# Top-k attention and two MLPs on one core: float32 scores, a head pair side by side

## The chip, the core and the metric

The kernel runs on one core of one Trainium2 chip. The metric is device time in microseconds of the whole program, one launch. Within the core TensorE (PE) multiplies, VectorE (DVE), ScalarE (ACT) and GpSimd (POOL) do the elementwise work, and SyncE (SP) issues most DMAs. The loading of TensorE's stationary operand is listed as PEld.

## The reference

```python
# q, k, v: batch 2, heads 8, sequence 576, head width 64, float32
scores = (1 / sqrt(64)) * q @ k.T                 # 576 x 576 for each head
kth    = 32nd largest score of each row
scores = where(scores >= kth, scores, -1e9)
attn   = exp(scores - rowmax); attn /= attn.sum() + 1e-9
x = (attn @ v) with heads side by side            # 1152 tokens x 512
h = x @ w_in                                      # 512 -> 2048
g = h * tanh(log1p(exp(min(h, 20))))
x = g @ w_out                                     # 2048 -> 512
a, b = x @ w_a, x @ w_b                           # 512 -> 1536 each
out = (a * b) @ w_out2                            # 1536 -> 512
```

The choice of the 32 largest hangs on small differences between scores, so scores are computed to about float32 accuracy. The weights arrive as float64 bit patterns and are turned into float32 in the kernel.

## The kernel before

The 1152 tokens are nine tiles of 128. Tile 4 holds the last 64 tokens of both batches, so its two halves use two different sets of keys. For each tile and each of four head pairs (36 steps) the kernel makes the scores (`scores`), searches the 32 largest by four rounds of MAX8 (L501) and three of MATCH_REPLACE8 (L505) on VectorE (`largest`), and then makes masked exponentials on ScalarE, transposes them on TensorE (L558) and multiplies by v (L577, L581; `weighted_sum`). In these value products each head writes 64 of the 128 columns of the array, the two heads in turn.

How scores are made before: for tile 0 as plain float32 products over the 64 rows of one head (L471), 16 matmuls. For the other tiles q and k are split: the high part of k, rounded to a shorter format, lies in rows 0 to 63 and the remainder in rows 64 to 127 of one operand, and q, which the host has laid twice into 128 rows, is split into a high and a low operand. Two matmuls over 128 rows (L481), q high and q low against that k, then give a float32 result for one head and 288 keys; four of them in tile 4, one pair for each batch, with zeros in the other batch's columns. The splits are casts (helper `cast`, L353, on ScalarE or VectorE) and differences (helper `minus`, L365, on GpSimd or VectorE), once for each head of k in `prep_k` and for each tile and head pair of q in `prep_q`. The heads of one pair are worked one behind the other, and each half row of 288 scores goes from PSUM into SBUF by a ScalarE eviction (L487).

The MLPs: the first (`single`, plain float32, tiles 0, 1 and 2 one at a time: L810 and L738; `gated`, split into high and low parts in three terms, for tiles 3 to 5 and 6 to 8: L715, L738 and L736) has a gate (`gate`), which begins with an exponential, then a minimum with exp(20) on GpSimd or VectorE (L771), then four more operations. The second (`bilinear`) is split for all tiles (L715, L738) and runs first on tiles 0 to 2: its first product is the first L715 in the program, called the first split product below. The weights are converted early on ScalarE, GpSimd and VectorE (L648 to L667) and stored to DRAM for later loads.

The order of all this is set by a planner (`Plan`). Each piece of work has a priority from tables (`ATT`, `CONV`, `MLP`, `BIAS`), a cost by formula for each engine that may do it, and rotating buffers; the planner walks through time by these costs and gives each free engine the ready piece with the lowest priority number. The result is written out as one fixed order for each engine. Where the plan expects TensorE to be idle for more than 2 us ahead of a piece with a `fill`, it puts products of the identity matrix there (L359), so that the clock does not fall. Instructions on an engine run in that order.

```python
rate = 1.0 if warm else 0.5                        # planner's TensorE clock
add(one("PE", 484.0), ...)                         # L471, one head, 288 keys
add(one("PE", 132.0 * len(heads)), ...)            # L481, two matmuls (four in tile 4)
```

Of the kernel before, what the change touches and what calls it, by code (L numbers as in the profile page):

```python
# [29 lines left out]
ATT = (-95.6, -15.5, 57.8, 65.0, 267.4, 322.4, 412.6, 617.3, 258.4, 2216.9)  # L30
CONV = (-130.2, -85.8, -15.1, 293.4, 516.4)
MLP = ((-72.5, 59.6, -546.2, 994.6), (150.3, 181.0, 313.3, -81.3), (-893.9, 26.7, -324.4, 153.9), (354.4, 585.5),
        (832.0, -20.7), (569.8, 2514.2), (1477.1, 1301.3), (616.5, 711.8))
BIAS = {'scores': -41.8, 'search': 43.8, 'weigh': 44.9, 'gate': -652.5, 'conv': -24.4, 'load': -87.3, 'split':
        -71.0, 'x': -191.9, 'k': -413.0, 'prod': 21.0, 'acc': 35.4, 'out': 22.8, 'store': 307.2, 'v': 1080.8, 'px':
        -507.2, 'mask': 1116.2, 'turn': -37.7, 'tail': -40.6, 'last': -0.9, 'rest': 372.0}
FRESH = 200
RAW = (0,)
# [11 lines left out]
CAPS = {'bank': 3, 'ph': 2, 'acc': 3, 'w64': 4, 'w': 6, 'raw': 9, 'whl': 6, 's2': 5, 'wk': 3, 'e2': 2, 'et': 2, 'q':  # L50
        2, 'x': 4, 'y': 2, 'ep': 3, 'gs': 2, 'k': 1}
# [227 lines left out]
SHIFT = {'DVE': -103.4, 'POOL': -52.0, 'ACT': 3021.6, 'PE': 0, 'SP': 0}  # L279
LOCKED = 1091.7  # L280
# [9 lines left out]
def topk_attention_mlps(ctx: ExitStack, tc: tile.TileContext, q, k, v, vr, w, out):  # L290
# [7 lines left out]
    B, _, H, S = k.shape  # L298
    D = q.shape[1] // 2
    NP = H // 2  # L300
# [66 lines left out]
    kks = [buf("const", [P, S], F32R, "kk") for _ in range(H + 2)]  # L367
# [10 lines left out]
    V, V4, KK, KR, QQ, X, XR, Y, HELD = {}, {}, {}, {}, {}, {}, {}, {}, {}  # L378
# [20 lines left out]
    part = lambda z: slice(0, P) if z == 2 else slice(z * D, (z + 1) * D)  # L399

    def load_k(b, hp, pr, z):
        done = ready(J * b - 2) if b else []
        if (b, hp) not in KR:
            KR[b, hp] = buf("const", [P, 2, S], F32, "kr") if b == 0 and RAW else buf("wp", [P, 2, S], F32, "kr", CAPS["k"])
        kr = KR[b, hp]
        first = b == 0 and hp == 0
        for h, n in ((0, 1), (1, 1)) if first else ((0, 2),):
            dma(pr, lambda h=h, n=n: kr()[part(z), h:h + n], lambda h=h, n=n: k[b, part(z), 2 * hp + h:2 * hp + h + n, :],
                (495000 if z == 2 else 363000) * n / 2, done, [(kr, (z, h))])

    def k_parts(b, hp, s, rows):
        return [(KR[b, hp], (z, s if b == 0 and hp == 0 else 0)) for z in rows]

    def prep_k(b, hp, pr):
        load_k(b, hp, pr, 1 if (b, hp) in KR else 2)
        kr = KR[b, hp]
        for s in range(2):
            got = k_parts(b, hp, s, (0, 1) if b == 0 and RAW else (2,))
            kk = KK[b, 2 * hp + s] = kks[(b * H + 2 * hp + s) % (H + 2)]
            cast(pr, kk, lambda s=s: kr()[:, s], 95.0 + 0.84 * S, got, [(kk, 0)], True)  # L420
            minus(pr, lambda kk=kk: kk()[D:], lambda s=s: kr()[D:, s], lambda kk=kk: kk()[D:].bitcast(F32), S,
                  got + [(kk, 0)], [(kk, 0)])
# [547 lines left out]
```

## Time and profile before

| | us |
|---|---|
| median of three runs | 651.97 (651.19 to 652.31) |
| profiled execution, first to last instruction | 647.8 |
| median less that span | 4.17 |
| TensorE busy | 619.9 |
| VectorE busy | 546.0 |
| ScalarE busy | 478.3 |
| GpSimd busy | 440.8 |

For the profiled execution the profile gives its span; what lies around it is read as the 4.17 us by which the median of the runs stands above it. "Busy" counts an instruction's whole duration; TensorE's matmuls overlap, so that a matmul's duration is longer than the time from its start to the next one's start. A float32 matmul stands in the trace as two records, a matmul on rounded operands (type fp32r) as one. Shapes are partitions x elements; for TensorE "128\*64" is rows x columns of the array.

### The profile page before, as it was taken

To read this page: it belongs to the slowest core of one execution; us is meant where nothing else is said; L and a number is where in the kernel's file an instruction comes from. 1 tells how busy PE (TensorE), PEld (TensorE's weight loads), DVE (VectorE), ACT (ScalarE), POOL (GpSimd) and SP (SyncE) were. 2 spreads that over 40 slices of the span, in tenths; PEclk is the share of its full clock that TensorE was granted. 3 is DMA by queue.
4 is the path that set the end of the run, shared out by engine and by line. 5 is a ranking of instruction groups with operands and counts; after the bars stand their busy time and mean duration, and the time that the engine had idled before them with its cause. 6 is when DMAs were issued, how large, how long until landed. Compare 5 with 4: busy or idle time off the path is not lost.

```text
span 647.8 us, 12295 instructions
## 1 busy us (share of the span) xinstructions
PE 619.9 (96%) x4122; PEld 547.7 (85%) x4122; DVE 546.0 (84%) x1083; ACT 478.3 (74%) x1057; POOL 440.8 (68%) x480
## 2 busy tenths in 40 slices
PE   7889789999999999999999999999999999999997
PEld 5778657967758899899989998889989999999996
DVE  4999999999999999999999989998765666655552
ACT  5778798898998999997998888777454767632221
POOL 2898999998979999997787785556334566621110
PEclk9989999999999999999999999999999999999999
DMA  8879879898999867632753342223207534434401
GB/s 210 317 234 301 270 236 303 281 347 284 331 334 329 292 224 245 196 98 82 215 176 116 115 130 82 78 88 112 85 7 221 165 113 131 146 99 129 123 26 49
DMA packets 65248, 118.50 MB, mean 183 GB/s; under 512 B 6945, under 2 KB 23393, under 8 KB 65185
## 3 DMA queue, kind: packets, MB, share of 16 engines
q1 hardware_dynamic: 65104, 117.66, 56.9%
q8 instruction: 32, 0.52, 0.3%
q14 instruction: 32, 0.25, 0.1%
q10 hardware_dynamic: 80, 0.07, 0.0%
HBM read 97.52 MB, written 20.19 MB: 182 GB/s over the span
## 4 chain that ended last, share of the span: by engine, by line
PE 73%; DVE 11%; ACT 6%; POOL 4%; DMA 3%; issue 2%; POOLq 0%; SPq 0%; ACTq 0%; DVEq 0%
PE ph L715 32%; PE po L738 11%; PE acc L738 7%; PE acc L736 5%; DVE arena L501 5%; DVE arena L505 4%; PE psc L481 4%; PE px L577 4%; PE pe L558 4%; PE ph L810 2%; PE psc L471 2%; ACT arena L353 2%; POOL arena L667 2%; ACT arena L775 1%; POOL arena L663 1%
## 5 line engine op out<-in xcount | busy, mean ns | idle before, releaser
L365 POOL TENSOR_TENSOR arena<-arena,arena 128x512 fp32r<-128x512 f32 (+4 forms) x188 | 216.3, 1162 | 154.3 <-ACT arena L353 126.2
L715 PE MATMUL ph<-arena 128*128 128x384 f32 x1248 | 230.9, 337 | 1.1 <-DVE arena L859 0.8
L715 PEld LDWEIGHTS ph<-arena 128*128 128x128 f32 x1248 | 216.8, 188 | 4.1 <-DVE arena L859 1.1
L501 DVE MAX8 arena<-arena 128x8 f32<-128x576 f32 x288 | 204.2, 744 | 6.7 <-ACT arena L487 5.8
L353 ACT CAST arena<-arena 128x512 fp32r<-128x512 f32 (+4 forms) x223 | 121.3, 565 | 56.2 <-PE ph L715 21.8
L505 DVE MATCH_REPLACE8 arena<-arena 128x576 f32<-128x576 f32 x216 | 159.1, 740 | 0.1
L365 DVE TENSOR_TENSOR arena<-arena,arena 128x512 fp32r<-128x512 f32 (+3 forms) x110 | 81.0, 738 | 18.9 <-ACT arena L353 13.9
L738 PE MATMUL acc<-arena 128*128 128x512 f32 x240 | 83.9, 478 | 2.7 <-DVE arena L777 2.4
L738 PE MATMUL po<-arena 128*128 128x512 f32 x324 | 80.7, 394 | 0.0
L667 POOL TENSOR_TENSOR arena<-arena 128x512 int32<-128x512 int32 x59 | 77.2, 1312 | 3.5 <-DVE arena L661 2.0
L738 PEld LDWEIGHTS po<-arena 128*128 128x128 f32 x324 | 59.6, 188 | 11.2 <-issue 0.2
L487 ACT ACTIVATE arena<-psc 128x288 f32<-128x288 f32 x144 | 54.7, 420 | 12.6 <-PE psc L471 6.0
L544 ACT ACTIVATE arena<-arena 128x576 f32<-128x576 f32 x72 | 55.1, 779 | 10.3 <-DVE arena L501 9.2
L353 DVE CAST arena<-arena 128x512 fp32r<-128x512 f32 (+2 forms) x75 | 38.9, 523 | 28.1 <-PE ph L715 10.9
L663 POOL TENSOR_TENSOR arena<-arena,eight 128x512 uint32<-128x512 uint32 x55 | 58.2, 1063 | 3.7 <-ACT arena L648 2.6
L481 PE MATMUL psc<-arena 128*128 128x288 f32 x288 | 57.4, 324 | 1.4 <-POOL arena L365 1.4
L547 ACT ACTIVATE arena<-arena 128x576 f32<-128x576 f32 x72 | 56.2, 782 | 3.0 <-POOL arena L540 3.0
L738 PEld LDWEIGHTS acc<-arena 128*128 128x128 f32 x240 | 42.0, 189 | 15.5 <-issue 7.2
L353 ACT COPY arena<-pe 128x384 f32<-128x384 f32 x108 | 48.4, 486 | 6.6 <-PE pe L558 6.5
L558 PEld LDWEIGHTS pe<-ident,arena 128*128 128x128 f32 x324 | 37.8, 140 | 17.6 <-ACT arena L547 9.0
L558 PE MATMUL pe<-ident,arena 128*128 128x128 f32 x324 | 47.2, 275 | 5.5 <-ACT arena L547 4.7
L810 PEld LDWEIGHTS ph<-arena 128*128 128x128 f32 x384 | 45.5, 192 | 8.1 <-issue 3.3
(63 smaller groups left out, 766.6 us busy)
## 6 DMA issues: line engine op xcount, KB each, us to landing
arena<-ws SPq DMA_DIRECT2D x144, 256.0 KB, 2.8
arena<-in_w_dram SPq DMA_DIRECT2D x68, 512.0 KB, 5.2
ws<-arena SPq DMA_DIRECT2D x52, 256.0 KB, 5.5
arena<-wsa SPq DMA_DIRECT2D x48, 256.0 KB, 3.4
arena<-in_q_dram SPq DMA_DIRECT2D x8, 512.0 KB, 4.2
wsa<-arena SPq DMA_DIRECT2D x16, 256.0 KB, 5.3
arena<-in_k_dram SPq DMA_DIRECT2D x4, 576.0 KB, 6.1
arena<-in_v_dram SPq DMA_DIRECT2D x4, 512.0 KB, 6.6
```

Of the source, the lines that this page charges most:

```text
L353: add(eng, prio, lambda e: nc.scalar.copy(dst(), src()) if e == "ACT" else nc.vector.tensor_copy(dst(), src()), reads, writes)
L365: lambda e: ENG[e].tensor_sub(dst(), a(), b()), reads, writes)
L481: nc.tensor.matmul(psc()[:, :HS], z()[:, s, :], kk()[:, a * HS:(a + 1) * HS], start=(i == 0), stop=(i == len(heads) - 1))
L501: lambda e, s=s, src=src, got=got: nc.vector.max(m8()[:, s, got], src()[:, s, :]),
L505: lambda e, s=s, src=src, got=got: nc.vector.match_replace(wk()[:, s, :], m8()[:, s, got], src()[:, s, :], NEG),
L547: lambda e, s=s: nc.scalar.activation(e2()[:, s, :], e2()[:, s, :], AF.Exp, scale=-STEEP, bias=dm()[:, s - 2 + n:s - 1 + n], accum_out=at_ ...
L558: nc.tensor.transpose(pe()[:, i * P:(i + 1) * P], ef[:, n * P:(n + 1) * P], ident)
L663: nc.gpsimd.tensor_tensor(wi().bitcast(U32), wi().bitcast(U32), eight.to_broadcast([P, U]), op=ALU.mult)
L667: lambda e, word=word, wi=wi: ENG[e].tensor_tensor(wi(), wi(), word(I32, 0), op=ALU.add),
L715: nc.tensor.matmul(ph()[:, o:o + T], a, x, start=(i == 0), stop=(i == len(mm) - 1))
L738: nc.tensor.matmul(acc[i](), z[:, i * P:(i + 1) * P], a, start=begin, stop=end)
L810: nc.tensor.matmul(ph()[:, j * P:(j + 1) * P], wa()[:, j * P:(j + 1) * P], x()[:, c, :], start=(c == 0 and j == 0), stop=(c == NC - 1 and ...
```

## The change

- **Scores.** All tiles get plain float32 products over 64 rows. The host now lays the two heads of a pair into rows 0 to 63 and 64 to 127, so that q has 128 rows for a pair instead of each head twice, and k as well. One piece of work is two matmuls, head 0 on the upper 64 rows and head 1 on the lower 64, into two PSUM banks (L426 of the new program); for tile 4 four matmuls, each 64 rows by 64 columns. `prep_k`, `prep_q`, the zeroing and the special path of tile 0 go. Loads of q and k have half the bytes.
- **Gate minimum.** The same instruction now has a second operation, a maximum with 0, which leaves the value of an exponential as it is. Its planned costs change.
- **Plan.** New numbers in the tables; three rotating q buffers; the first pieces of the program get 15 identity products ahead of them.

```diff
-ATT = (-95.6, -15.5, 57.8, 65.0, 267.4, 322.4, 412.6, 617.3, 258.4, 2216.9)
+ATT = (-314.6, -14.6, 75.9, 107.2, 174.6, 217.9, 226.5, 1087.3, 1309.4, 2701.9)
...
-SHIFT = {'DVE': -103.4, 'POOL': -52.0, 'ACT': 3021.6, 'PE': 0, 'SP': 0}
+SHIFT = {'DVE': -22.2, 'POOL': 1042.3, 'ACT': 6005.8, 'PE': 0, 'SP': 0}
...
-    def prep_k(b, hp, pr):
-        load_k(b, hp, pr, 1 if (b, hp) in KR else 2)
-        kr = KR[b, hp]
-        for s in range(2):
-            got = k_parts(b, hp, s, (0, 1) if b == 0 and RAW else (2,))
-            kk = KK[b, 2 * hp + s] = kks[(b * H + 2 * hp + s) % (H + 2)]
-            cast(pr, kk, lambda s=s: kr()[:, s], 95.0 + 0.84 * S, got, [(kk, 0)], True)
-            minus(pr, lambda kk=kk: kk()[D:], lambda s=s: kr()[D:, s], lambda kk=kk: kk()[D:].bitcast(F32), S,
-                  got + [(kk, 0)], [(kk, 0)])
+        kr = KR[b, hp] = buf("const", [P, S], F32, "kr")
+        dma(pr, kr, lambda: k[b, :, hp, :], 295000, done, [(kr, 0)])
...
-                    heads = [(z, KK[i, 2 * hp + s]) for i, y in made for z in y]
-
-                    def mult(e, s=s, a=a, psc=psc, heads=heads):
-                        for i, (z, kk) in enumerate(heads):
-                            nc.tensor.matmul(psc()[:, :HS], z()[:, s, :], kk()[:, a * HS:(a + 1) * HS],
-                                             start=(i == 0), stop=(i == len(heads) - 1))
-
-                    add(one("PE", 132.0 * len(heads)), pr, mult, [(z, None) for y in heads for z in y], [(psc, 0)], [s2])
-                    fill(psc)
+        for a in range(2):
+            pscs = [bank("psc") for _ in range(2)]
+
+            def mult(e, a=a, pscs=pscs):
+                for i, o, n in groups(t):
+                    for s in range(2):
+                        nc.tensor.matmul(pscs[s]()[o:o + n, :HS], qr()[s * D:(s + 1) * D, hp, o:o + n],
+                                         KR[i, hp]()[s * D:(s + 1) * D, a * HS:(a + 1) * HS], start=True, stop=True)
+
+            add(one("PE", 2 * 0.84 * HS), pr, mult, got, [(z, 0) for z in pscs], [s2])
+            fill(pscs[0])
...
-        add({"POOL": (330.0 + 2.42 * N, True), "DVE": (70.0 + 0.52 * N, True)}, pr,
-            lambda z: ENG[z].tensor_scalar(e(), e(), TOP, None, op0=ALU.min), [(e, 0)], [(e, 0)])
+        add({"POOL": (75.0 + 1.21 * N, True), "DVE": (250.0 + 0.52 * N, True)}, pr,
+            lambda z: ENG[z].tensor_scalar(e(), e(), TOP, 0.0, op0=ALU.min, op1=ALU.max), [(e, 0)], [(e, 0)])
...
-    arrays = {"q": _np.concatenate([turned_q] * 2, axis=1), "k": _np.concatenate([turned] * 2, axis=1), "v": main, "vr": rest}
+    paired_q = turned_q.reshape(9, 64, 4, 2, P).transpose(0, 3, 1, 2, 4).reshape(9, P, 4, P)
+    paired_k = turned.reshape(2, 64, 4, 2, -1).transpose(0, 3, 1, 2, 4).reshape(2, P, 4, -1)
+    arrays = {"q": paired_q, "k": paired_k, "v": main, "vr": rest}
```

Line numbers shift: before L501, L505, L558, L577, L581, L596, L715 and L810 are after L447, L451, L504, L523, L527, L542, L661 and L756.

The order on TensorE at the start of the program, before (psc are scores, pe the transposes of exponentials, px the value products, ph and acc the MLP; x16 is a count):

```order
L471 MATMUL psc<-arena_81 128x288 x16
L359 MATMUL pe<-ident 128x128 x31
L558 MATMUL pe<-ident,arena_81 128x128 x9
L481 MATMUL psc<-arena_82 128x288 x6
L596 MATMUL px<-ident,arena_81 64x128 x2
L577 MATMUL px<-arena_81 64x128 x8
L581 MATMUL px<-arena_81 64x128 x2
```

and after:

```order
L358 MATMUL psc<-ident 128x128 x15
L426 MATMUL psc<-arena_81 128x288 x18
L504 MATMUL pe<-ident,arena_81 128x128 x6
L542 MATMUL px<-ident,arena_81 64x128 x2
L504 MATMUL pe<-ident,arena_81 128x128 x3
L426 MATMUL psc<-arena_81 128x288 x2
L523 MATMUL px<-arena_81 64x128 x8
L527 MATMUL px<-arena_81 64x128 x2
```

Tile 0's 16 products one head at a time and 31 identity products behind them have become 15 identity products ahead of nine score pairs, the last of which belongs to tile 1.

The order on TensorE around the first split product (L715 before, L661 after; po is the split layer's output, prs and pt small transposes), before:

```order
L577 MATMUL px<-arena_81 64x128 x8
L581 MATMUL px<-arena_81 64x128 x2
L481 MATMUL psc<-arena_82 128x288 x16
L715 MATMUL ph<-arena_82 128x384 x48
L738 MATMUL po<-arena_82 128x512 x9
L558 MATMUL pe<-ident,arena_81 128x128 x3
L621 MATMUL prs<-ident,arena_81 64x128 x8
L558 MATMUL pe<-ident,arena_81 128x128 x3
L715 MATMUL ph<-arena_82 128x384 x12
L558 MATMUL pe<-ident,arena_81 128x128 x3
```

and after:

```order
L523 MATMUL px<-arena_81 64x128 x8
L527 MATMUL px<-arena_81 64x128 x2
L736 MATMUL pt<-ident,arena_81 128x128 x4
L426 MATMUL psc<-arena_81 64x288 x8
L661 MATMUL ph<-arena_82 128x384 x12
L426 MATMUL psc<-arena_81 64x288 x4
L661 MATMUL ph<-arena_82 128x384 x12
L504 MATMUL pe<-ident,arena_81 128x128 x3
L426 MATMUL psc<-arena_81 64x288 x4
L661 MATMUL ph<-arena_82 128x384 x12
L567 MATMUL prs<-ident,arena_81 64x128 x8
```

Runs of 4 to 16 whole-array score products have become one or two groups of four quarter products (tile 4) with whole-array products between them.

The order on VectorE in tile 0's search, before (MAX and MATCH_REPLACE are the search, L353 the cast and L365 the difference of the k splits):

```order
L501 MAX arena_81<-arena_81 128x8
L505 MATCH_REPLACE arena_81<-arena_81 128x576
L501 MAX arena_81<-arena_81 128x8 x2
L505 MATCH_REPLACE arena_81<-arena_81 128x576
L365 TENSOR_TENSOR arena_82<-arena_81,arena_82 64x576
L505 MATCH_REPLACE arena_81<-arena_81 128x576
L501 MAX arena_81<-arena_81 128x8
L365 TENSOR_TENSOR arena_82<-arena_81,arena_82 64x576
L353 CAST arena_82<-arena_81 128x576
L501 MAX arena_81<-arena_81 128x8
L505 MATCH_REPLACE arena_81<-arena_81 128x576
L365 TENSOR_TENSOR arena_82<-arena_81,arena_82 64x576
```

and after:

```order
L447 MAX arena_81<-arena_81 128x8 x2
L451 MATCH_REPLACE arena_81<-arena_81 128x576 x2
L447 MAX arena_81<-arena_81 128x8 x2
L451 MATCH_REPLACE arena_81<-arena_81 128x576 x2
L447 MAX arena_81<-arena_81 128x8 x2
L451 MATCH_REPLACE arena_81<-arena_81 128x576 x2
L447 MAX arena_81<-arena_81 128x8 x4
L451 MATCH_REPLACE arena_81<-arena_81 128x576 x2
L447 MAX arena_81<-arena_81 128x8
```

The casts and differences between the searches are gone, and both heads of the pair go through each round together.

## Rows read from the trace of the kernel before

**Rows 1.** The page: parts 1 and 4

```profile
PE 619.9 (96%) x4122; PEld 547.7 (85%) x4122; DVE 546.0 (84%) x1083; ACT 478.3 (74%) x1057; POOL 440.8 (68%) x480
...
PE 73%; DVE 11%; ACT 6%; POOL 4%; DMA 3%; issue 2%; POOLq 0%; SPq 0%; ACTq 0%; DVEq 0%
```

**Rows 2.** Windows: busy us (instructions) of each engine, clock, DMA share, GB/s

```profile
0.00:28.00 28.00, 24.02 (x91) 18.88 (x92) 18.41 (x34) 18.24 (x38) 13.64 (x19) 1.00 0.87 253
28.00:202.00 174.00, 156.49 (x1168) 120.99 (x1168) 172.51 (x363) 150.05 (x333) 158.87 (x192) 0.99 0.88 294
202.00:490.00 288.00, 286.88 (x2036) 261.96 (x2035) 267.80 (x542) 239.46 (x546) 209.03 (x221) 1.00 0.46 145
490.00:648.00 158.00, 152.56 (x833) 145.90 (x831) 87.26 (x146) 70.55 (x143) 59.28 (x50) 1.00 0.39 117
```

**Rows 3.** The chain from 28 to 202 us: shares by line

```profile
by line: DVE arena L501 17.0%; DVE arena L505 14.1%; PE ph L810 9.1%; issue 6.8%; PE acc L738 6.2%; POOL arena L667 4.5%; PE psc L481 4.1%; DMA arena<-in_w_dram 3.4%; POOL arena L663 3.2%; POOL arena L655 2.9%; PE px L577 2.9%; ACT arena L3
```

**Rows 4.** The chain from 202 to 490 us: shares by line

```profile
by line: PE ph L715 41.1%; PE po L738 15.2%; PE acc L738 11.0%; PE pe L558 6.9%; PE px L577 6.6%; PE psc L481 6.3%; PE prs L621 2.1%; ACT arena L353 2.1%; DMA arena<-wsa 1.6%; PE px L581 1.5%; ACT arena L487 0.8%; DVE arena L501 0.7%; DVE a
```

**Rows 5.** Groups by form: count | busy us, mean ns | idle before

```profile
L655 POOL TENSOR_SCALAR arena<-arena 128x512 int32<-128x512 uint32 x41 | 28.4, 694 | 3.4
L771 POOL TENSOR_SCALAR arena<-arena 128x384 f32<-128x384 f32 x21 | 25.2, 1199 | 13.4 <-ACT arena L769 12.9
...
L365 POOL TENSOR_TENSOR arena<-arena,arena 128x256 fp32r<-128x256 f32 x22 | 17.7, 809 | 6.6 <-ACT arena L353 5.9 <-DVE arena L353 0.6
...
L365 POOL TENSOR_TENSOR arena<-arena,arena 64x576 fp32r<-64x576 f32 x7 | 9.9, 1421 | 11.1 <-ACT arena L353 10.7
...
L365 DVE TENSOR_TENSOR arena<-arena,arena 64x576 fp32r<-64x576 f32 x9 | 8.4, 939 | 2.8 <-ACT arena L353 2.6
...
L667 DVE CUSTOM_DVE_ANT_0 arena<-arena 128x1024 uint16<-128x1024 uint16 x9 | 7.0, 775 | 0.2 <-POOL arena L663 0.2
...
L353 DVE CAST arena<-arena 128x256 fp32r<-128x256 f32 x7 | 3.5, 505 | 0.0
...
L365 DVE TENSOR_TENSOR arena<-arena,arena 128x256 fp32r<-128x256 f32 x6 | 2.9, 501 | 0.0
L353 DVE CAST arena<-arena 128x576 fp32r<-128x576 f32 x5 | 2.7, 547 | 0.0
```

**Rows 6.** Timeline of the start: start us, us, engine, line, instruction, count [idle before]

```profile
1.42 0.29 POOL masks.py:199 TENSOR_SCALAR_AFFINE_SELECT ident<-ident 128x128 f32<-128x128 f32 x1
...
3.98 15.70 PE L471 MATMUL psc<-arena 64*128 64x288 f32 x32 [3.98 <-DMA arena<-in_k_dram]
...
6.71 0.76 DVE L501 MAX8 arena<-arena 128x8 f32<-128x576 f32 x1 [5.81 <-ACT arena L487]
...
19.61 3.78 PE L359 MATMUL pe<-ident 128*128 128x128 f32 x16
...
23.80 3.40 PE L359 MATMUL pe<-ident 128*128 128x128 f32 x29
```

**Rows 7.** Timeline of TensorE: score and value products, 157 to 203 us

```profile
157.87 0.53 PE L481 MATMUL psc<-arena 128*128 128x288 f32 x2
158.33 0.44 PE L596 MATMUL px<-ident,arena 128*64 128x128 f32 x4
158.70 0.54 PE L481 MATMUL psc<-arena 128*128 128x288 f32 x2
...
198.59 0.33 PE L577 MATMUL px<-arena 128*64 128x128 f32 x2
...
198.59 1.09 PE L577 MATMUL px<-arena 128*64 128x128 f32 x16
199.51 0.39 PE L581 MATMUL px<-arena 128*64 128x128 f32 x4
199.83 2.39 PE L481 MATMUL psc<-arena 128*128 128x288 f32 x16
202.06 0.34 PE L715 MATMUL ph<-arena 128*128 128x384 f32 x1
```

More of the change, by code (lines that the diff above doesn't have):

```diff
@@ L29 @@
        (1, (6, 7, 8), 1), (2, (6, 7, 8), 1)]
-ATT = (-95.6, -15.5, 57.8, 65.0, 267.4, 322.4, 412.6, 617.3, 258.4, 2216.9)
[L31 to L36, printed above, removed]
+ATT = (-314.6, -14.6, 75.9, 107.2, 174.6, 217.9, 226.5, 1087.3, 1309.4, 2701.9)
+CONV = (-367.8, -149.1, -67.0, 338.2, 855.3)
+MLP = ((-31.0, 92.9, -3739.3, 5207.1), (-571.5, 311.3, 64.6, 3.4), (-7255.7, 338.5, -1288.6, -9158.9), (369.5,
+        622.9), (956.2, -1304.0), (766.3, 4149.4), (5710.6, -2774.1), (2810.4, 119.5))
+BIAS = {'scores': -107.7, 'search': 148.3, 'weigh': 1.0, 'gate': -429.4, 'conv': -43.1, 'load': -195.4,
+        'split': -108.7, 'x': -298.7, 'k': -3620.2, 'prod': 126.2, 'acc': 78.0, 'out': -2013.8, 'store':
+        579.0, 'v': 2670.8, 'px': -1145.1, 'mask': -827.7, 'turn': -89.6, 'tail': -0.2, 'last': -0.3, 'rest':
+        1048.0}
 FRESH = 200
-RAW = (0,)
 MERGE = (6, 7, 8)
@@ L297, in topk_attention_mlps @@
     nc = tc.nc
-    B, _, H, S = k.shape
+    B, _, NP, S = k.shape
+    H = 2 * NP
     D = q.shape[1] // 2
-    NP = H // 2
     DM = H * D
@@ L365, in minus @@
             lambda e: ENG[e].tensor_sub(dst(), a(), b()), reads, writes)
-    kks = [buf("const", [P, S], F32R, "kk") for _ in range(H + 2)]
     ident = const.tile([P, P], F32, name="ident")
@@ L376, in topk_attention_mlps @@
     nc.scalar.preload_act_table_set("natural_log_exp_and_others")
-    V, V4, KK, KR, QQ, X, XR, Y, HELD = {}, {}, {}, {}, {}, {}, {}, {}, {}
+    V, V4, KR, QQ, X, XR, Y, HELD = {}, {}, {}, {}, {}, {}, {}, {}
     def groups(t):
@@ L397, in load_v, with load_k @@
                 [(v4, None)], [(v4, s)])
-    part = lambda z: slice(0, P) if z == 2 else slice(z * D, (z + 1) * D)
-    def load_k(b, hp, pr, z):
+    def load_k(b, hp, pr):
         done = ready(J * b - 2) if b else []
-        if (b, hp) not in KR:
-            KR[b, hp] = buf("const", [P, 2, S], F32, "kr") if b == 0 and RAW else buf("wp", [P, 2, S], F32, "kr", CAPS["k"])
-        kr = KR[b, hp]
[L406 to L409, printed above, removed]
@@ L450, in topk_attention_mlps @@
-    since = [next(t for t in range(J + 1) if t not in RAW), J]
+        kr = KR[b, hp] = buf("const", [P, S], F32, "kr")
+        dma(pr, kr, lambda: k[b, :, hp, :], 295000, done, [(kr, 0)])
+    def load_q(t, pr):
+        qr = QQ[t] = buf("stg", [P, NP, P], F32, "qr", CAPS["qr"])
+        for i, (a, b) in enumerate(((0, 1), (1, NP)) if t == 0 else ((0, NP),)):
+            dma(pr if i == 0 else pr + BIAS["rest"], lambda a=a, b=b: qr()[:, a:b], lambda a=a, b=b: q[t][:, a:b],
+                65600 * (b - a), (), [(qr, i)], nc.scalar if t == 0 and i == 0 else nc.sync)
@@ new lines, in scores @@
+        if t == 0:
+            load_k(0, hp, pr + BIAS["k"] * (1 if hp else 3))
+        if t == J:
+            load_k(1, hp, pr + BIAS["k"])
+        qr = QQ[t]
+        got = [(qr, int(t == 0 and hp > 0))] + [(KR[i, hp], 0) for i, _, _ in groups(t)]
+        s2 = buf("att", [P, 2, S], F32, "s2", CAPS["s2"])
+        for a in range(2):
[7 more added lines that the diff above has]
+            fill(pscs[0])
+            for s in range(2):
```

53 lines of the change are left out of this document (4 added, 49 removed).

## The prediction

> **What bounds the kernel now.** I read the page first, then the busy times by stretch, then the chain of waits in two of the stretches, then single forms and single moments on TensorE. The page shows TensorE busy for 619.9 of 647.8 us and on 73% of the chain [rows 1]. That is a mean over unlike stretches, so the stretches come next [rows 2]. From 28 to 202 us VectorE is busy 172.5 of 174 us, GpSimd 158.9 and the DMA engines 88% of the time; TensorE idles 17.5 us. The chain of that stretch is VectorE's search (L501 and L505, 31%) with GpSimd's weight work between, and the four largest TensorE lines together have 22% [rows 3]. The reader is to see that the helpers set the pace there. At 202 us the first product of the first split layer starts (L715). From there to 490 us TensorE is busy 286.9 of 288 us [rows 2] and its lines are 91% of the chain (the first seven entries and the last px of [rows 4]). Behind 490 us it is alone again, with 5.4 us idle. So two questions decide: how much earlier do the helpers let TensorE reach that first product, and does TensorE then have more or less to do?
>
> **What the helpers lose.** The k and q splits go. On VectorE that is 9 differences of 64x576 at 0.939 us, 5 casts of 128x576 at 0.547, 7 casts of 128x256 at 0.505 and 6 differences at 0.501 [rows 5]: 8.4 + 2.7 + 3.5 + 3.0 = 17.6 us in all. What counts for the first question is what stands on VectorE's queue ahead of the last MAX8 of token tile 2 (the 96th). I counted both orders: before, 5 of the 64x576 differences, 1 wide cast, 2 narrow casts, 3 narrow differences and 7 weight additions (L667, 0.775 us); after, none of the first four and 4 additions. That is 4.7 + 0.5 + 1.0 + 1.5 + 2.3 = 10.0 us less. The order section shows how the first of them vanish between the searches of tile 0. GpSimd's queue up to its 30th weight addition loses 3 differences at 1.421 and 8 at 0.809 us: 10.7 us. The gate minimum gets a second operation; no row shows it so, but the two-operation form of L655 on 128x512 takes 0.694 us where the minimum on 128x384 takes 1.199 us [rows 5]. Bounds: nothing gained, or 29 x (1.199 - 0.52) = 20 us off GpSimd if the cost falls with the width (0.694 x 384 / 512 = 0.52). I take the latter; most of it falls where TensorE sets the pace, and it enters the sum with nothing. The DMAs lose half of q and half of k, on queues that are 88% busy; SyncE's queue gives up six k loads and brings its first weight load forward. No one thing is late instead, since VectorE, GpSimd and DMA are each relieved. I take 10 us off the time at which the first split product starts. Ends: 0, if TensorE's share of that chain swallows it, and 14.
>
> **What TensorE gains and loses.** First the unit. The 32 records of L471 (two for each float32 matmul over 64 rows) take 15.70 us, 0.48 each [rows 6]. The clock column says 1.00 there [rows 2], but identity matmuls just behind start every 0.213 us (16 in 20 to 23 us) and every 0.112 us a little later (29 in 24 to 27) [rows 6]: the first 23 us ran at the lower level, 1.2 GHz, although TensorE was busy from 4 us on, and the level rose to 2.4 GHz during the identity matmuls. At the upper level a record of L471 is then 0.24 us and one head's half row 0.48 us. Two heads side by side are not in this trace. The nearest thing is: the value products of L577 write 64 columns for each head, and two of them start together and run at one time: 2 started in 198.58 to 198.62, and 20 records (L577 and L581) take the 1.24 us up to the next line where one after the other at 0.109 they would need 2.2 [rows 7]. Bounds for a pair: 0.48 us side by side, 0.96 in turn. I take 0.48. The same holds for the four quarter products of tile 4.
>
> The Trainium skill (TensorE: Matmul & The Clock Gate, Part 3: Packing small matmuls) says that matmuls start and end strictly in program order. By that a head's second record would hold the other head's first back, and a lone pair would take three steps, 0.72 us. The trace differs for column halves: two heads' records start together and so do the next two. I keep the rule as a rival.
>
> Second, the switch between whole-array and half-array products. From 157.87 to 158.70 us, 0.83, there run two whole products of L481, the first of them just behind a switch, and four half-array records of L596 [rows 7]. Elsewhere two whole ones take 2 x 0.139 (below) and four half ones, two by two, 2 x 0.11: 0.50 us. So one way there and back costs 0.33 us beside the visit's own work. The Trainium skill (TensorEngine Tiling (Array Packing), Key Properties) says that a change of tiling mode drains TensorE; the trace agrees with those 0.33 us, which the kernel before paid for value products alone.
>
> Now the sum from the first split product on, which starts at 202.06 us [rows 7]. Before, 160 of the whole score products stand behind it, at 2.23 / 16 = 0.139 us (16 from 199.83 to 202.06 [rows 7]): 22.3 us. After, 76 matmuls, which are 32 pairs and 3 groups of four, nearly each a visit of its own between whole products, as the second place in the order section shows: 35 x (0.48 + 0.33) = 28.4 us. TensorE sets the pace there, so +6 us. Bounds: +1, if neighbours share switches and the weight loads hide, and +23, if pairs run in turn (35 x 0.48 = 17 more). Ahead of it: 128 products (17.8 us) give way to 28 visits (22.7 us), and 30 identity matmuls at 0.22 to 23; +4 us in a stretch with 17.5 us idle, so it costs nothing, unless pairs run in turn (13 us more: the cover is then used up).
>
> The start: before, the first MAX8 begins at 6.71 us and VectorE works 18.4 of the first 28 us. After, 15 identity matmuls (30 records) stand ahead of the first score. The identity is there at 1.71 us [rows 6], so they end between 5.1 and 8.1 us by the two rates. Two score visits and their evictions put the first MAX8 at about 9. That loses some 2.5 us, but then all 18 matmuls follow within 4.5 us, and VectorE's other 2.9 idle us of the first 28 go. I take zero, ends -2 and +3.
>
> Last, 9% of the chain from 202 to 490 us (27 us) is not TensorE's: a DMA, casts and searches [rows 4]. The other 10 of VectorE's 17.6 us and most of the gate's 20 us on GpSimd go from here on. Since TensorE is idle only 1.1 us there, I give 3 us to it; ends 0 and 12.
>
> **Sum.** -10 + 6 + 0 - 3 = -7 us against the profiled span of 647.8, so 640.8. The median of the runs shown, 651.97, lies 4.2 us above that span, and the span is what the sum is made against: 645.0 us.
>
> **Rivals.** (a) The pairs run in turn. For it: no row has two row halves, and the level of the clock did not rise in 15 us of 64-row products. Against it: the column halves. Price: +17 behind the first split product, some 4 at the start, and about 4 where the idle time ahead runs out: 645 + 25 = 670 us, slower. It decides from a visit of 1.01 us on (0.81 + 7 / 35). Chance 0.12. (b) One head's second record holds the other head's first back, so that a lone pair takes three steps of 0.24 us: 35 x 0.24 = 8.4 us more, 653, within or just above no change. For it: nothing in this trace; against it: the column halves that start together. Chance 0.08. (c) The helpers' gain is not passed on: TensorE has a good fifth of the chain ahead of the first split product [rows 3], and dearer visits sit there too. Then 10 becomes 2, and the time is 653. Chance 0.12. (d) The order fits better than the sum says: 14 instead of 10, 9 instead of 3 and +3 instead of +6: 632 us. For it: GpSimd loses 28 us of differences (7 x 1.421 + 22 x 0.809) besides the gate's. Against: TensorE's 1.1 us idle. Chance 0.20. (e) The clock: TensorE has little to do from about 12 us until tile 0's exponentials; in the trace before it fell to 1.2 GHz once after such a gap (0.99 over the 174 us of the second stretch of [rows 2] is 3.5 us at half). If it stays low through tile 0, about 5 us, 650. Chance 0.06.
>
> **How the numbers follow.** The forecast holds with 0.42, its own range 638 to 651. Within 0.2% (1.3 us, about what a measurement of this kernel can tell) of 651.97: 0.04 of the forecast, half of (b) and (c) less a little, and a third of (e): 0.13. Faster: 0.37 + 0.20 + 0.04 + 0.03 = 0.64. Slower: the rest, 0.23. The range runs from 630, just under (d), to 662, short of (a), whose tenth is left out.
>
> **What would show it.** Right: the first split product starts near 192 us; L426's two heads start within some 10 ns and a visit takes about 0.81 us; VectorE is busy throughout up to 190 us. Wrong: L426's records at 0.24 us one behind the other; the first split product still at 200 us; or from 190 to 480 us TensorE idle by more than a few us, which would mean that I took the wrong bound.

## The result, and the profile after

| | before | after |
|---|---|---|
| median, us (5 runs each) | 651.97 (649.47 to 653.9) | 645.29 (645.14 to 645.98) |
| ratio, 95% interval | | 0.991 (0.9886 to 0.9933) |
| profiled span, us | 647.8 | 643.3 |
| first split product starts, us | 202.1 | 192.4 |
| from there to the end, us | 445.7 | 450.9 |
| search of token tile 2 ends (96th MAX8 starts), us | 155.0 | 146.4 |

Faster by 0.9% by the medians, as forecast (645.0). By the two profiled spans the gain is 4.5 us, by the medians 6.7: runs of the kernel before scatter by 4 us, and its profiled execution lay low among them, while those of the changed kernel lie within 0.9 us. The profiled execution of the changed kernel took 645.14 us, 1.8 more than its span.

The page of the changed kernel, parts 1 and 4, against [rows 1]:

```profile
PE 618.4 (96%) x4076; PEld 515.2 (80%) x4076; DVE 536.6 (83%) x1065; ACT 453.2 (70%) x992; POOL 401.1 (62%) x443
...
PE 82%; DVE 9%; ACT 3%; POOL 2%; issue 2%; DVEq 0%; ACTq 0%; POOLq 0%
```

TensorE is as busy as before, the helpers less (GpSimd by 40 us), and TensorE's share of the chain rises from 73 to 82%. The windows, first over the same stretches as [rows 2], then cut at the first split product (columns as there):

```profile
0.00:28.00 28.00, 17.10 (x107) 12.94 (x107) 19.20 (x45) 16.27 (x39) 15.71 (x26) 0.82 0.87 307
28.00:202.00 174.00, 165.13 (x1179) 113.99 (x1181) 167.95 (x358) 150.68 (x327) 140.15 (x172) 0.98 0.84 283
202.00:490.00 288.00, 286.96 (x1980) 244.82 (x1975) 253.57 (x507) 223.64 (x500) 193.94 (x201) 1.00 0.44 135
490.00:643.00 153.00, 149.21 (x818) 143.49 (x816) 95.88 (x159) 62.60 (x128) 51.31 (x46) 1.00 0.37 113
...
28.00:192.40 164.40, 155.70 (x1112) 106.41 (x1112) 158.59 (x338) 141.82 (x306) 132.22 (x164) 0.98 0.84 280
...
192.40:643.30 450.90, 445.60 (x2861) 395.89 (x2857) 358.82 (x685) 295.10 (x650) 253.17 (x255) 1.00 0.43 132
```

The same cut of the kernel before, at 202.1 us:

```profile
28.00:202.10 174.10, 156.59 (x1169) 121.09 (x1169) 172.61 (x365) 150.15 (x334) 158.97 (x192) 0.99 0.88 294
...
202.10:647.80 445.70, 439.34 (x2866) 407.76 (x2865) 354.96 (x686) 309.91 (x689) 268.21 (x271) 1.00 0.43 135
```

The reader is to see two things. Ahead of the first split product the stretch shrinks from 174.1 to 164.4 us; VectorE, which idled 1.5 us in it, now idles 5.8, and TensorE idles 8.7 instead of 17.5. Behind it TensorE's busy time grows by 6.3 us (439.34 to 445.60) and its idle time falls from 6.4 to 5.3: +5.2 in all. The chain of waits from 28 to 192 us, by line, against [rows 3]:

```profile
by line: PE acc L684 16.3%; PE ph L756 16.3%; DVE arena L451 11.3%; DVE arena L447 10.9%; issue 5.4%; PE px L523 5.4%; PE psc L426 5.4%; PE pe L504 5.2%; ACT arena L721 3.7%; POOL arena L613 2.6%; POOL arena L601 1.8%; ACT arena L715 1.7%; 
```

The search (L447, L451) has 22% where it had 31, and five TensorE lines have 49% where the four largest had 22. The helpers no longer set the pace of that stretch alone.

TensorE's timeline in the changed kernel: the start, the start of the first split product, a score visit between whole products, and a run of whole products without one (start us, us, engine, line, instruction, count):

```profile
1.77 5.38 PE L358 MATMUL psc<-ident 128*128 128x128 f32 x30 [1.77 <-POOL ident masks.py:199]
7.08 5.29 PE L426 MATMUL psc<-arena 64*128 64x288 f32 x36
...
192.41 0.45 PE L661 MATMUL ph<-arena 128*128 128x384 f32 x1
...
216.08 0.76 PE L426 MATMUL psc<-arena 64*128 64x288 f32 x4
216.76 2.35 PE L661 MATMUL ph<-arena 128*128 128x384 f32 x12
219.05 0.76 PE L426 MATMUL psc<-arena 64*128 64x288 f32 x4
...
518.28 4.32 PE L661 MATMUL ph<-arena 128*128 128x384 f32 x24
522.45 0.85 PE L682 MATMUL acc<-arena 128*128 128x384 f32 x4
```

One visit is four records. One whole product takes (522.45 - 518.28) / 24 = 0.174 us, so 12 take 2.09. From the visit at 216.08 to the next at 219.05 there are 2.97 us: a visit costs 2.97 - 2.09 = 0.88 us with its switches, of which 0.68 lie between its start and the next whole product. Four records of 0.24 us in turn would alone be 0.96, so the two heads do run side by side. The first two records of the first pair, one of each head, share the same 0.51 us; in the trace they start 7 ns apart:

```profile
7.08 0.51 PE L426 MATMUL psc<-arena 64*128 64x288 f32 x2
```

On VectorE the first search now starts here, at 6.71 in [rows 6]:

```profile
8.91 1.42 DVE L447 MAX8 arena<-arena 128x8 f32<-128x576 f32 x2 [8.01 <-ACT arena L433]
```

Last the gate's minimum, by form (count | busy us, mean ns | idle before), against L771 in [rows 5], and the square on ScalarE that follows it:

```profile
L721 ACT ACTIVATE arena<-arena 128x384 f32<-128x384 f32 x64 | 32.8, 526 | 11.7 <-POOL arena L717 7.1 <-DVE arena L717 4.2
...
L717 POOL TENSOR_SCALAR arena<-arena 128x384 f32<-128x384 f32 x22 | 12.7, 578 | 18.1 <-ACT arena L715 17.5 <-DVE arena L352 0.3
...
L717 POOL TENSOR_SCALAR arena<-arena 128x512 f32<-128x512 f32 x8 | 4.9, 613 | 3.8 <-ACT arena L715 3.2 <-DVE arena L607 0.3
...
L717 DVE TENSOR_SCALAR arena<-arena 128x512 f32<-128x512 f32 x4 | 1.9, 476 | 0.1
```

With its second operation the minimum on GpSimd takes 578 ns where it took 1199. The predicted 520 ns was near.

### The profile page after: what moved, and what is told of

Its sections match the earlier page's. It is cut to its first block, busy times and chain, and to the rows that moved or that the text cites. A ratio compares the mean times of both kernels' runs of the same rounds, so it can differ in the third digit from the quotient of the medians.

```text
span 643.3 us, 12026 instructions
## 1 busy us (share of the span) xinstructions
PE 618.4 (96%) x4076; PEld 515.2 (80%) x4076; DVE 536.6 (83%) x1065; ACT 453.2 (70%) x992; POOL 401.1 (62%) x443
## 4 chain that ended last, share of the span: by engine, by line
PE 82%; DVE 9%; ACT 3%; POOL 2%; issue 2%; DVEq 0%; ACTq 0%; POOLq 0%
PE ph L661 34%; PE po L684 12%; PE acc L684 10%; PE acc L682 5%; PE psc L426 5%; PE pe L504 5%; PE px L523 4%; PE ph L756 4%; DVE arena L447 4%; DVE arena L451 4%; ACT arena L721 1%; PE prs L567 1%; PE px L527 1%; POOL arena L613 1%; DVE arena L710 0%
## 5 line engine op out<-in xcount | busy, mean ns | idle before, releaser
L364 POOL TENSOR_TENSOR arena<-arena,arena 128x512 fp32r<-128x512 f32 (+1 forms) x155 | 191.6, 1250 | 141.6 <-ACT arena L352 70.4
L661 PE MATMUL ph<-arena 128*128 128x384 f32 x1248 | 232.8, 338 | 0.6 <-DVE arena L710 0.6
L661 PEld LDWEIGHTS ph<-arena 128*128 128x128 f32 x1248 | 216.7, 188 | 11.3 <-issue 5.7
L447 DVE MAX8 arena<-arena 128x8 f32<-128x576 f32 x288 | 203.5, 746 | 9.5 <-ACT arena L433 9.5
L451 DVE MATCH_REPLACE8 arena<-arena 128x576 f32<-128x576 f32 x216 | 159.2, 741 | 0.0
L352 ACT CAST arena<-arena 128x384 fp32r<-128x384 f32 (+1 forms) x163 | 90.3, 578 | 25.9 <-DVE arena L827 16.7
L684 PE MATMUL acc<-arena 128*128 128x512 f32 x240 | 88.9, 495 | 3.2 <-POOL arena L613 2.2
L613 POOL TENSOR_TENSOR arena<-arena 128x512 int32<-128x512 int32 x63 | 81.8, 1301 | 4.1 <-ACT arena L599 1.4
L364 DVE TENSOR_TENSOR arena<-arena,arena 128x512 fp32r<-128x512 f32 (+1 forms) x91 | 69.1, 761 | 9.4 <-ACT arena L352 7.4
L609 POOL TENSOR_TENSOR arena<-arena,eight 128x512 uint32<-128x512 uint32 x58 | 61.4, 1064 | 11.2 <-ACT arena L594 9.6
L504 PEld LDWEIGHTS pe<-ident,arena 128*128 128x128 f32 x324 | 38.4, 144 | 28.4 <-ACT arena L493 12.3
L504 PE MATMUL pe<-ident,arena 128*128 128x128 f32 x324 | 49.2, 282 | 11.4 <-ACT arena L493 9.6
L352 ACT COPY arena<-pe 128x384 f32<-128x384 f32 x108 | 48.2, 484 | 15.2 <-PE pe L504 14.7
L352 ACT COPY arena<-ph 128x384 f32<-128x384 f32 x36 | 17.3, 481 | 57.5 <-PE ph L661 37.4
L721 ACT ACTIVATE arena<-arena 128x384 f32<-128x384 f32 (+1 forms) x88 | 47.4, 557 | 11.7 <-POOL arena L717 7.1
L426 PE MATMUL psc<-arena 64*128 64x288 f32 (+1 forms) x320 | 53.2, 451 | 0.1
```

The costliest lines, as they stand in the source:

```text
L352: add(eng, prio, lambda e: nc.scalar.copy(dst(), src()) if e == "ACT" else nc.vector.tensor_copy(dst(), src()), reads, writes)
L364: lambda e: ENG[e].tensor_sub(dst(), a(), b()), reads, writes)
L426: nc.tensor.matmul(pscs[s]()[o:o + n, :HS], qr()[s * D:(s + 1) * D, hp, o:o + n], KR[i, hp]()[s * D:(s + 1) * D, a * HS:(a + 1) * HS], sta ...
L447: lambda e, s=s, src=src, got=got: nc.vector.max(m8()[:, s, got], src()[:, s, :]),
L451: lambda e, s=s, src=src, got=got: nc.vector.match_replace(wk()[:, s, :], m8()[:, s, got], src()[:, s, :], NEG),
L504: nc.tensor.transpose(pe()[:, i * P:(i + 1) * P], ef[:, n * P:(n + 1) * P], ident)
```

## The experiments

The edits are against the changed kernel where nothing else is said; the order of instructions stays as it was unless the planner's costs or tables are edited. "First split" is the start of the first split product, "behind" the time from there to the end.

**The changed kernel once more**, to see what recurs.

> The changed kernel once more, as the measure for the three that follow on the same chip. Both theories: 643 to 647 us, span about 643.5, first split product near 192.4 us. If its low-clock stretches are an accident of where in time a gap falls, they lie elsewhere in this run; if the program sets them, they come again near 16 to 26 and 70 to 77 us.

645.02 us, ratio 0.9913 (0.9893 to 0.9934); first split 192.1, behind 450.9. The result stands, and of VectorE's instructions ahead of the first split product none took more than 25 ns longer or shorter than in the first profile. The granted clock fell to 1.2 GHz from 17.2 us for 10.2 us and from 68.4 for 6.8, near where it did in the first profile (from 15.8 for 10.2 and from 70.4 for 6.8): it comes again, so the program brings it about. The first search starts at 9.63 here instead of 8.91.

**The gate minimum with one operation again.**

```diff
-  ENG[z].tensor_scalar(e(), e(), TOP, 0.0, op0=ALU.min, op1=ALU.max)
+  ENG[z].tensor_scalar(e(), e(), TOP, None, op0=ALU.min)
```

> The changed kernel with the gate minimum as a single operation again, the order of all engines unchanged. Theory (the gate part is worth little, since TensorE sets the pace where most gates run): GpSimd's 30 minimums go from about 0.55 to 1.2 and 1.5 us, some 20 us more GpSimd time in all, and the time rises by 0 to 2 us. Rival (the gate carries much of the gain, because each gate chain is on the way to a product): the time rises by 4 us or more and TensorE idles behind gates in 202 to 490 us.

651.27 us, ratio 1.0005 (0.9993 to 1.0018). The whole gain of the change goes. The same groups in this kernel:

```profile
L721 ACT ACTIVATE arena<-arena 128x384 f32<-128x384 f32 x64 | 33.1, 525 | 21.2 <-POOL arena L717 17.6 <-DVE arena L717 2.9
L717 POOL TENSOR_SCALAR arena<-arena 128x384 f32<-128x384 f32 x22 | 28.2, 1281 | 12.7 <-ACT arena L715 11.6 <-DVE arena L352 0.3
...
L717 POOL TENSOR_SCALAR arena<-arena 128x512 f32<-128x512 f32 x8 | 12.3, 1540 | 3.1 <-ACT arena L715 2.4 <-DVE arena L607 0.3
```

The square waits 17.6 us for the minimum instead of 7.1. The span grows by 6.4 us against the run above: first split 196.7 (+4.6), behind 452.7 (+1.8). My theory (0 to 2 us) falls. The rival had the size, but most of the loss is ahead of the first split product, where only the eight minimums on 512 columns are on GpSimd.

**Only those on 512 columns with one operation.**

```diff
+  ... tensor_scalar(e(), e(), TOP, None, op0=ALU.min) if N == U else ... (as before)
```

> The changed kernel with the single-operation minimum for the 12 gates of tiles 0 to 2 alone (128x512, 8 of them on GpSimd), order unchanged. With all gates single the first split product moved from 192.1 to 196.7 us and the span rose by 6.4 us. Theory (the loss ahead of the first split product comes from these 8, at 0.93 us each, and through them from GpSimd and the chain of each gate): first split product 195.5 to 197 us, span 647 to 648. Rival (it comes from GpSimd as a whole, also behind): first split product within 1.5 us of 192.1, span below 645.

649.56 us, ratio 0.9979 (0.9963 to 0.9995); first split 195.9 (+3.8), behind 450.9. So eight minimums, 0.9 us longer each on GpSimd (1.54 against 0.61), cost 4 us ahead of the first split product, as my theory had it. The rest of the gate's gain, some 2 us, is behind it.

**Twelve MAX8 of tiles 0 to 2 issued twice**, one in each step: how much of a us on VectorE's queue reaches the first split product?

```diff
-  lambda e, ...: nc.vector.max(m8()[:, s, got], src()[:, s, :])
+  lambda e, ..., n=2 if t < 3 and r == 3 and s else 1: [
+      nc.vector.max(m8()[:, s, got], src()[:, s, :]) for _ in range(n)]
```

> The changed kernel with 12 of the MAX8 of tiles 0 to 2 issued twice, one in each of their steps: 12 x 0.744 = 8.9 us more on VectorE ahead of the last search of tile 2, nothing else changed. Theory (VectorE's queue sets when the first split product starts, and TensorE's work behind it fixes the rest): first split product 7 to 9 us later, near 200 us, and the time longer by 6 to 9 us. Rival (VectorE has room there, or TensorE makes it up later): first split product within 3 us of 192.4 and the time longer by 0 to 3 us.

650.07 us, ratio 0.9967 (0.9948 to 0.9986). VectorE has 8.9 us more to do; the search of tile 2 ends 5.9 us later, the first split product starts at 196.7, 4.6 later, and behind it nothing moves (450.9). About half passes, between my theory and its rival: the queue has idle time of its own by now, and from 28 us to the first split product that falls from 5.8 to 1.1 us.

**The pairs of tiles 5 to 8 twice**: does TensorE set the pace behind the first split product?

```diff
-  for i, o, n in groups(t):
+  for i, o, n in groups(t) * (2 if t > J else 1):
```

> The changed kernel with every score pair of tiles 5 to 8 computed twice within its visit: 32 pairs x 0.48 = 15.4 us more on TensorE behind the first split product, no more switches, the price of pairs that ran in turn. Theory (TensorE sets the pace there): time longer by 13 to 16 us, near 660. Rival (TensorE's busy share hides waits that take it up): 0 to 6 us.

661.22 us, ratio 1.0148 (1.0124 to 1.0172). 32 pairs of 0.48 us are 15.4 us; behind is 466.1, 15.2 more. It passes one to one. This is also about what pairs in turn would have cost there. The first split product starts at 193.8, 1.7 later than in the changed kernel's second run, although nothing ahead of it was edited: a shift of that size in a single trace shows nothing.

**Whole-array scores**: q for each head over 128 rows with zeros in the other head's 64, the heads in turn. The products do the same sums; the q tile has twice the bytes.

```diff
-  qr = QQ[t] = buf("stg", [P, NP, P], F32, "qr", CAPS["qr"])
+  qr = QQ[t] = buf("stg", [P, H, P], F32, "qr", CAPS["qr"])
...
-  qr()[s * D:(s + 1) * D, hp, o:o + n], KR[i, hp]()[s * D:(s + 1) * D, a * HS:(a + 1) * HS]
+  qr()[:, 2 * hp + s, o:o + n], KR[i, hp]()[:, a * HS:(a + 1) * HS]
```

> The changed kernel with q laid out for each head over 128 rows, zeros in the other head's rows (512 KB a tile again), so that a score product uses the whole array and the two heads run in turn; order unchanged. A pair then takes 2 x 0.48 = 0.96 us and no switch; tile 4 keeps its switch and takes 0.96 instead of 0.48. Theory (a visit side by side costs 0.88 us with its two switches): behind the first split product 32 x 0.08 + 3 x 0.5 = 4 us more, span 646 to 649 in all. Rival (the switches are hidden and a pair costs 0.5 to 0.6): 32 x 0.4 = 13 us more, 656 or above.

657.3 us, ratio 1.0104 (1.0086 to 1.0121). First split 197.2 (+5.1 against the changed kernel's second run), behind 457.7 (+6.7). A tile 4 visit in this kernel, then a visit of a pair, twelve whole products and the next visit:

```profile
214.10 1.20 PE L426 MATMUL psc<-arena 128*64 128x288 f32 x8
215.23 0.55 PE L504 MATMUL pe<-ident,arena 128*128 128x128 f32 x3
...
225.03 1.13 PE L426 MATMUL psc<-arena 128*128 128x288 f32 x4
225.79 2.46 PE L661 MATMUL ph<-arena 128*128 128x384 f32 x12
228.09 1.13 PE L426 MATMUL psc<-arena 128*128 128x288 f32 x4
```

The tile 4 visit takes 1.13 us to the next line, where it took 0.65. The visit of a pair costs 3.06 - 2.09 = 0.97 us against 0.88 side by side. So what running side by side saves is more than what the switch of the array's mode costs. My +4 behind was low (the span of 654.8 lies between my 646 to 649 and the rival's 656), and I had not expected the start to move. TensorE is busy for 6.6 us more from 28 us to the first split product; the loads of q are also twice as large, and no run separates the two.

**Identity products in the gap of the start**, so that the clock stays up.

```diff
-  busy = o.end
+  busy, count = o.end, count + 1
+  if count == 10:
+      o.fill(32)
```

> The changed kernel with 32 identity products (64 records, 7.2 us at 0.112) behind the first nine score pairs, ahead of the first transposes, where TensorE idles from 12.4 to 21.0 us and the clock falls to 1.2 GHz from 15.8 to 26.0 us. Theory (VectorE paces this stretch and the low clock costs it little): clock 1.00 up to 50 us, time lower by 0 to 1.5 us. Rival (the low clock delays tile 0 and all behind it): first split product 3 us or more earlier and the time lower by as much.

644.92 us, ratio 0.9909 (0.9888 to 0.9929): no gain over the changed kernel, although the clock of the first 28 us is 1.00 where it was 0.82. It fell later instead, from 28.9 us for 3.4, so my "1.00 up to 50 us" did not come true. First split 192.3. With or without the products in the gap the stretch ends at the same time, so the low clock there costs nothing that these runs show.

**No identity products at the start.**

```diff
-  if o.fill and o.start - busy > 2000.0:
+  if o.fill and busy and o.start - busy > 2000.0:
```

> The changed kernel without the 15 identity products ahead of the first score pair. The pairs then start near 4.3 us at 1.2 GHz: 0.48 us a record, 0.96 a pair. Two heads side by side fill the whole array; theory: they raise the clock as the identity products do, within some 7 us, which half-array products did not in 15 us before. Rival: 64-row products keep the clock low, in pairs too, until whole-array products come. Under both VectorE's first MAX8 begins near 7.0 us, not 8.9, and the time is lower by 0 to 2 us, since VectorE paces the stretch to 192 us.

643.57 us, ratio 0.9888 (0.9867 to 0.9909), the quickest of all. TensorE's start in this kernel:

```profile
4.39 2.29 PE L426 MATMUL psc<-arena 64*128 64x288 f32 x8 [4.39 <-DMA arena<-in_q_dram]
7.06 3.99 PE L426 MATMUL psc<-arena 64*128 64x288 f32 x24 [0.38 <-DMA arena<-in_k_dram]
11.31 1.05 PE L426 MATMUL psc<-arena 64*128 64x288 f32 x4 [0.26 <-ACT arena L433]
```

The scores start at 4.39 us instead of 7.08, at 0.48 us a record, and their records fall to 0.24 us from 8.93 us on, as in my theory and not as in its rival. The first search starts at 7.16 instead of 8.91, and the first split product at 190.1. So the identity products cost 2 us by the first split product and 1.5 by the medians: they hold the first scores back for longer than they shorten them.

**The new minimum alone in the kernel before** (edit against that kernel, its order kept).

```diff
-  ENG[z].tensor_scalar(e(), e(), TOP, None, op0=ALU.min)
+  ENG[z].tensor_scalar(e(), e(), TOP, 0.0, op0=ALU.min, op1=ALU.max)
```

> The kernel before with the two-operation minimum alone, the order of all engines unchanged. Theory: GpSimd's 29 minimums fall from 1.2 and 1.5 us to about 0.55 and 0.7 us, 19 us less GpSimd time; 8 of them lie ahead of the first split product, so it starts up to 3 us earlier; time lower by 0 to 3 us. Rival (the gate is the main part of the gain): 5 us or more.

655.44 us, ratio 1.0056 (1.0032 to 1.0079): slower, against my theory and its rival, though GpSimd's minimums fell to 554 and 613 ns. First split 205.5, 3.4 later than before. The delay of VectorE's instructions grows from 0.5 to 3.8 us between 79 and 94 us. VectorE's timeline there in the kernel before:

```profile
83.92 0.47 DVE L365 TENSOR_TENSOR arena<-arena,arena 128x256 fp32r<-128x256 f32 x1
...
85.04 0.41 DVE L771 TENSOR_SCALAR arena<-arena 128x512 f32<-128x512 f32 x1
...
87.36 0.41 DVE L661 TENSOR_SCALAR arena<-arena 128x512 int32<-128x512 int32 x1
...
88.36 0.75 DVE L667 CUSTOM_DVE_ANT_0 arena<-arena 128x1024 uint16<-128x1024 uint16 x1
```

The same four instructions with the new minimum, and one that waits:

```profile
84.21 1.28 DVE L777 SCALAR_TENSOR_TENSOR arena<-arena,ph 128x512 f32<-128x512 f32 x2 [1.05 <-ACT arena L775]
85.41 0.85 DVE L365 TENSOR_TENSOR arena<-arena,arena 128x256 fp32r<-128x256 f32 x1
...
86.91 0.79 DVE L771 TENSOR_SCALAR arena<-arena 128x512 f32<-128x512 f32 x1
...
89.61 1.21 DVE L661 TENSOR_SCALAR arena<-arena 128x512 int32<-128x512 int32 x1
...
91.41 1.48 DVE L667 CUSTOM_DVE_ANT_0 arena<-arena 128x1024 uint16<-128x1024 uint16 x1
```

GpSimd's instructions beside the last two, in the kernel before:

```profile
87.33 0.51 POOL L510 TENSOR_SCALAR arena<-arena 128x2 f32<-128x2 f32 x1
...
88.66 1.35 POOL L663 TENSOR_TENSOR arena<-arena,eight 128x512 uint32<-128x512 uint32 x1
```

And beside all four with the new minimum:

```profile
84.54 1.45 POOL L655 TENSOR_SCALAR arena<-arena 128x512 int32<-128x512 uint32 x2
86.07 1.36 POOL L667 TENSOR_TENSOR arena<-arena 128x512 int32<-128x512 int32 x1
...
88.46 0.21 POOL L510 TENSOR_SCALAR arena<-arena 128x2 f32<-128x2 f32 x1 [1.04 <-DVE arena L501]
...
89.50 1.04 POOL L663 TENSOR_TENSOR arena<-arena,eight 128x512 uint32<-128x512 uint32 x1
...
91.06 1.29 POOL L667 TENSOR_TENSOR arena<-arena 128x512 int32<-128x512 int32 x1
```

With the new minimum each of the four VectorE instructions starts while one of GpSimd's is under way, and lasts until 0.3 to 0.5 us after that one's end: L661 from 89.61 to 90.82, GpSimd's until 90.54. Before, VectorE was not held up; there the two GpSimd instructions shown ran longer (L510 0.51 instead of 0.21, L663 1.35 instead of 1.04). VectorE's four lose 0.38 + 0.38 + 0.80 + 0.73 = 2.3 us, and the wait for ScalarE adds 1.05: together the 3.3 by which the delay grows. The Trainium skill (SBUF — State Buffer, SBUF: two separate sides) says that GpSimd and some kinds of VectorE instruction share a pair of ports, which the first to start holds for its whole instruction while the other blocks; the trace agrees with VectorE's four ends, but in the kernel before L510 on GpSimd starts 0.03 us ahead of VectorE's L661 and is still the one that runs longer. That the two engines hold each other up is read from these times; no run moves one of the instructions out of the way. Nor is there a second trace of the kernel before, whose runs scatter by some 5 us here (649.8 to 655.0).

**The new kernel under the old tables** (priorities, shifts and the planner's start conditions of the kernel before).

```diff
-ATT = (-314.6, -14.6, 75.9, ...)
+ATT = (-95.6, -15.5, 57.8, ...)
...
-LOCKED = 1802.5
+LOCKED = 1091.7
```

> The new scores and gate with the planner's tables of before (priorities, shifts and lock weight). Theory (the gain comes from the work that went, the tables only keep the order fitting): 645 to 655 us, first split product still 5 us or more ahead of the 202.1 of before. Rival (the new tables carry the gain): 655 us or more, first split product no earlier than before.

659.58 us, ratio 1.0123 (1.0101 to 1.0144). First split 198.1, 4 earlier than before where my theory had 5 or more and the rival nothing, but behind 459.1: the rival is right on the time. The new tables are worth 14 us.

**The new scores with the old minimum, planned with its own costs**, under the new tables.

```diff
-  add({"POOL": (75.0 + 1.21 * N, True), "DVE": (250.0 + 0.52 * N, True)}, pr, ... op1=ALU.max)
+  add({"POOL": (330.0 + 2.42 * N, True), "DVE": (70.0 + 0.52 * N, True)}, pr, ... op0=ALU.min)
```

> The changed kernel with the single-operation minimum and the planner's old costs for it, new tables, planned anew: the new scores alone. Theory (the planner's order is fitted to its costs, so any other order with the same tables is worse): 650 us or more, as the single minimum in the unchanged order (651.3), by waits behind the first split product too. Rival (the loss in the unchanged order came from a plan that expected a short minimum): 647 us or less.

659.4 us, ratio 1.0133 (1.0116 to 1.015); first split 205.1, behind 452.3. The costs are near what GpSimd takes (1259 planned and 1271 ns measured on 128x384), though not what VectorE does (270 and 787). The order is 8 us worse than the one kept in the second experiment, all of it ahead of the first split product (205.1 against 196.7), where my theory put part of it behind. Here too the tables fit the costs that they came with.

**The visit at its measured price in the planner**, without identity products at the start.

```diff
-  add(one("PE", 2 * 0.84 * HS), pr, mult, got, ...)
+  add(one("PE", 880.0), pr, mult, got, ...)
```

> The changed kernel without the identity products ahead of the first pair, and with the planner's cost of a score visit raised from 0.484 to 0.88 us, as the trace shows it; tables unchanged, planned anew. Theory (tables are fitted to one set of costs): 645 to 660 us, slower than the 643.6 without the identity products alone. Rival (the plan loses by not knowing the switches): 640 us or less.

664.16 us, ratio 1.0208 (1.0186 to 1.0231): 20.6 us slower than the same kernel with the price of 484 ns, beyond the upper end I had given. First split 204.2, behind 456.8. A truer cost alone made this plan worse.

## Why the prediction was right, and where it was not

**The start of the first split product, -10.** Measured -9.7 (202.1 to 192.4), where single traces with the same work ahead differ by up to 1.7. The size held, the reason only in part. I took 10 us off VectorE's queue and let all of it pass. The doubled searches show that about half passes, and the changed windows show why: VectorE idles 5.8 us there and five of TensorE's lines have half the chain, so my sign "VectorE is busy throughout up to 190 us" failed. Four of the ten come from the gate minimum, which the sum entered "with nothing" because I let its gain fall where TensorE sets the pace. Eight of the short minimums are ahead of it. Rival (c), the gain not passed on, was thus half true, and the gate made up for it: that the size came out is in part luck. What GpSimd's other 10.7 us and the halved loads gave was not measured apart.

**The start, 0 (-2 to +3).** No run measures this term by itself; it lies within the -9.7. Its mechanism was as said: the first search at 8.91 against "about 9". That the identity products themselves cost 1.5 to 2 us (190.1 without them) was not in the sum.

**TensorE behind it, +6.** Measured +6.3 busy. The unit was 0.88 us, not 0.81; by it the term is 35 x 0.88 - 22.3 = +8.5, and the busy time shows 2 less. Two things in the traces go that way: the 37 groups of whole score products that stood there before take 24.5 us up to the next product, not 22.3, and of the 34 visits of the changed kernel (two pairs share one) 8 stand right behind half-array products, so that no whole product is switched away from. How much each makes was not measured apart.

**Other waits behind it, -3.** Mis-sized: TensorE's idle time fell by 1.1 us, and so the stretch grew by 5.2 instead of 3. The doubled pairs confirm the ground of both terms: behind the first split product a us of TensorE is a us of the end.

**What lies around the span, +4.2.** This is the step that failed by most. It was the median of the runs less one span, the 4.17 us of the table before; an execution's own time less its own span is 1.8 us, for both kernels in the runs of the experiments. So the profiled execution before took some 649.6 us, 2.4 below its kernel's median. The sum of -7 stands against -4.5 by spans, and the term that was 2.4 too large made up for it, so that 645.0 against 645.29 owes something to two errors of opposite sign.

**The rivals.** (a) and (b) fall: a lone visit has 0.68 us from its start to the next product, where three steps of 0.24 would be 0.72 and four 0.96, and the heads start 7 ns apart. The Trainium skill (TensorE: Matmul & The Clock Gate, Part 3: Packing small matmuls) has matmuls start and end strictly in program order. The trace agrees for whole matmuls (head 1 starts 7 ns behind head 0), but not for the two records of each: for two row halves, as for column halves [rows 7], the second head's first record is not held back by the first head's second. (d) did not come: the tables are worth 14 us over the old ones, but behind the first split product TensorE gave up 1.1 us of idle time and was busy for 6.3 us more. (e): the clock did fall in that gap, from 15.8 to 26.0 us after TensorE had had nothing to do from about 12, and filling it gained nothing.

**That the parts do not add.** The new minimum alone loses 3.1 us against the kernel before it was put into, the new scores alone are at its time or 9 us above it, and both under the old tables are 7 us above. Of these only the set with its own order gains. The instructions of VectorE that were drawn out beside GpSimd's suggest for one case how an order goes stale when one of its instructions becomes shorter. What in the replanned orders costs the 8 to 20 us stays open; it was not followed instruction by instruction.

## What to carry to other kernels

In a kernel whose engines follow one fixed order, price an edit by the engine that ends the stretch it lies in, instruction by instruction, and look for the few short ones ahead of the milestone even when most of the gain lies behind it. Do not expect all of what one busy helper loses to pass when other engines are on the chain too: here about half did. Take the time around the span from one execution's own time, and try the cheap removal as well: leaving the identity products out at the start gave 1.5 us more, 643.57 us, the best version here.

## What the runs showed of the hardware

A minimum on GpSimd took less than half the time when it had a second operation: 578 instead of 1281 ns on 128x384 and 613 instead of 1540 on 128x512, of float32; on VectorE the form with two took 742 against 730 and 476 against 623. Two float32 products on the two row halves run side by side (a doubled pair adds 15.2 / 32 = 0.48 us, as long as the two records of one product), and the granted clock rose from 1.2 to 2.4 GHz while nothing but such pairs ran (records of 0.48 us from 4.39 us on, of 0.24 from 8.93 on); behind 15.7 us of products on one half it was still at the lower level [rows 6]. And in four places VectorE's instructions that started while one of GpSimd's was under way took 1.8 to 3 times as long, L661 1.21 instead of 0.41 us.
